# Attention on TensorE: which operand of the key-value products stands, and which moves

## The chip, the cores and the metric

The kernel runs on one core of a Trainium2 chip. The metric is the device time of one execution in microseconds (us). Before the change the median of three runs is 1320.67 us (1320.23 to 1321.27).

## The reference

Linear attention with exponential features, followed by two feed-forward mixtures that the change doesn't touch. Batch 4, 8 heads, 576 positions, head size 64, 128 features:

```python
def phi(x):
    proj = np.einsum('bhsd,df->bhsf', x, w_phi)
    proj = proj - np.max(np.abs(proj), axis=-1, keepdims=True)
    return np.concatenate([np.exp(proj), np.exp(-proj)], axis=-1)
q_p, k_p = (phi(q), phi(k))
kv = np.einsum('bhsf,bhsd->bhfd', k_p, v)
z = np.sum(k_p, axis=2)
num = np.einsum('bhsf,bhfd->bhsd', q_p, kv)
den = np.einsum('bhsf,bhf->bhs', q_p, z)[..., None] + 1e-06
return (num / den).astype(np.float32)
```

So each head needs a table kv (256 features by 64 values) and the sums z (256) of the key exponentials over all positions. All is f32.

## The kernel before, in words

The 32 heads are worked in 16 pairs. A pair's 576 positions are four blocks of 128 and a tail of 64; the tails of both heads share one tile. Per pair, TensorE projects keys and queries (`project`, L403, and `project_tails`, L410), VectorE finds the largest magnitude and subtracts it (`largest` L419, `less` L425), ScalarE takes both exponentials of the keys with positions on the partitions (`exp_keys` L430, `exp_tails` L435, tiles ke and ket). The queries are transposed on TensorE first (`turn_queries`, L500 and L503) and exponentiated with features on the partitions (`exp_queries`, L509 and L511, tile qe).

The key-value table comes in these steps:

- `key_values` (L447): 32 columns of v stand in one of four column strips of the array (two heads, two halves of the 64 values), the 256 exponentials of one block move. Values end on the partitions, features in the columns, in a PSUM tile kv of its own. It is issued in two parts (plan names KV-0 and KV-1).
- `sum_keys` (L470, L471; plan name Z): GpSimd or VectorE adds the four blocks of exponentials into zsum.
- `add_up` (L456; ZZ): ones stand and zsum and ket move, so the sums land beside the table.
- `save_kv` (L209 by the copy helper; CV): two copies of 256 columns out of PSUM into kvs.
- `turn_kv` (L484, L486; TV): four transposes on TensorE, since attention needs features on the partitions.
- `copy_kv` (L209; VH) and `add_halves` (L493; VZ): a copy of 384 columns to kvt, and an addition of two halves of the sums.

`attend` (L522; A) and `denominators` (L532; AD) take 32 columns of kvt as the standing operand and move qe. A chain on VectorE and ScalarE (D0 to X2) divides and writes Xh and Xl, the input of the first mixture. Blocks of that mixture (U and M, L292 and L313) are mixed into attention's order as soon as their input is there. The rest of the mixtures follows attention.

Instructions are issued by a planner (`Plan.run`). TensorE's order is the list ORDER, written out by hand; each entry is one step such as KV3-1. The other engines' orders come from the planner's booked costs, due times (RANK and SHIFT) and buffers; a step that two engines can do goes to the one that would end first by these costs. `SWITCH` holds the planner's booked costs for a change of array mode: row (two strips of 64 rows), quarter (four strips of 32 columns), full (f32 on the whole array) and rounded (fp32r on the whole array). Loads are issued from the DMA queue of SyncE in the planner's order (`load`, L390 to L394); v has one buffer of 128 x 512, vt two. PSUM has five shared banks (bank), one for kv and two for the mixture (mm).

Of the kernel before, what the change touches and what calls it, by code (L numbers as in the profile page):

```python
# [45 lines left out]
NZ = 0  # L46
# [10 lines left out]
    C=-146.759, CV0=109.999, CV1=-182.316, D0=-57.584, D1=-146.332, D2=39.304, D3=-224.318, E0=88.966,  # L57
    E1=41.132, E2=96.018, G0=208.743, G1=-173.239, G2=438.049, I=-129.377, N0=-51.099, N1=-127.846, Rk0=-43.022,
    Rk1=162.626, Rq0=-5.647, Rq1=132.286, Rt=-62.242, Sk0=-113.184, Sk1=7.061, Sq0=-463.551, Sq1=-197.328,
    St=-302.881, VH=16.756, VZ=-249.208, W=41.842, W3=73.288, W4=140.933, W5=-142.37, X0=255.513, X1=364.708,  # L60
    X2=383.376, Z0=266.794, Z1=165.123, ldk=-63.631, ldq=-41.539, ldv=10.731,
# [6 lines left out]
AD2 ZZ3 T3-1 TV3 Pk-4 A2-0 AD3 A2-1 PT4 Pq-4 Pk-5 A3-0 KV4-0 KV4-1 A3-1 Pq-5 ZZ4 T4-0 T4-1 TV4 KV5-0 T4-2
T5-0 T5-2 KV5-1 A4-0 A4-1 AD4 PT6 Pk-6 ZZ5 T5-1 U2-0 TV5 Pq-6 KV6-0 A5-0 KV6-1 AD5 A5-1 T6-0 T6-2 PT7 ZZ6
PT8 Pk-7 Pq-7 TV6 U0-0 T7-0 T6-1 U3-0 T7-1 T7-2 KV7-0 AD6 A6-0 KV7-1 PT9 ZZ7 Pk-8 Pq-8 TV7 U1-0 A6-1 A7-0  # L70
KV8-0 A7-1 KV8-1 AD7 ZZ8 Pk-9 Pq-9 T8-0 M0-1 T8-1 M0-3 TV8 T9-0 T8-2 T9-1 KV9-0 PT11 A8-0 AD8 KV9-1 PT10 ZZ9
T9-2 M0-2 M0-0 Pk-10 Pq-10 TV9 U2-1 U3-1 A8-1 AD9 KV10-0 A9-0 KV10-1 A9-1 ZZ10 Pk-11 Pq-11 T10-0 U0-1 TV10
T10-1 T11-0 U1-1 T11-2 T10-2 T11-1 KV11-0 PT13 KV11-1 AD10 ZZ11 Pq-12 Pk-12 TV11 M1-1 M1-3 M1-2 A10-0 PT12
KV12-0 A10-1 AD11 A11-0 KV12-1 A11-1 ZZ12 Pk-13 Pq-13 T12-0 M1-0 T12-1 T13-0 TV12 U3-2 T12-2 T13-1 T13-2
KV13-0 AD12 KV13-1 PT14 ZZ13 A12-0 Pq-14 Pk-14 TV13 U1-2 U0-2 U2-2 KV14-0 A12-1 KV14-1 PT15 ZZ14 AD13 Pk-15
Pq-15 T14-0 M2-3 M2-0 T14-2 T14-1 TV14 KV15-0 A13-0 KV15-1 A13-1 ZZ15 A14-0 TV15 T15-0 T15-1 T15-2 AD14
# [997 lines left out]
```

## Time and profile before

| | us |
|---|---|
| median of three runs | 1320.67 |
| the profiled execution, its own time | 1321.2 |
| its span, first to last instruction | 1319.1 |
| from the start to the end of attention's matmuls | 236.7 |

The profile is one execution. PE is TensorE's matmuls, PEld its weight loads, DVE VectorE, ACT ScalarE, POOL GpSimd, SP SyncE with the DMA queue. Matmuls overlap, so the busy time of PE is the time in which at least one is in flight, and the price of one is the distance from its start to that of the next. "128*32" is the part of the array an instruction uses (rows by columns), "128x256" the operand that moves, or, of a load, the operand that stands. An f32 matmul call is two loads and two matmul instructions.

### The profile page before, as it was taken

The numbers are of one execution on the slowest core, as the hardware profiler recorded it, in microseconds if no ns is written. First come the engines' busy times: TensorE is split into PE (matmuls) and PEld (weight loads), VectorE is DVE, ScalarE is ACT, GpSimd is POOL, SyncE is SP. The second block draws the span as 40 slices with busy tenths as digits, with TensorE's granted clock in tenths as the row PEclk, the third lists the DMA queues.
The fourth block names the chain that finished last, engine by engine and source line by source line (L and its number), as shares of the span: only waits on it lengthen the run. The fifth ranks groups of instructions, "written<-read, shape, count | busy, mean of one in ns | idle before, by whom it ended". The sixth has DMA issues, their size and how long they took to land.

```text
span 1319.1 us, 21240 instructions
## 1 busy us (share of the span) xinstructions
PE 1307.2 (99%) x8184; PEld 1118.5 (85%) x8184; DVE 758.1 (57%) x1283; ACT 454.6 (34%) x979; POOL 274.2 (21%) x292
## 2 busy tenths in 40 slices
PE   9999999999999999998999999999999999999998
PEld 5577776888888888897999998999999899999997
DVE  7996866999697456664455446433343453333433
ACT  6775655332131121253444433222222232222221
POOL 5562412120020130274566620000000000000000
PEclk9999999999999999999999999999999999999999
DMA  5431220322020030098677666666666565566641
GB/s 168 123 110 49 55 56 12 112 81 96 17 72 9 9 119 1 25 320 287 246 254 257 251 221 197 227 188 194 195 188 192 176 224 175 176 186 190 192 135 48
DMA packets 102469, 192.36 MB, mean 146 GB/s; under 512 B 13920, under 2 KB 14048, under 8 KB 102368
## 3 DMA queue, kind: packets, MB, share of 16 engines
q1 hardware_dynamic: 102368, 191.00, 44.5%
q8 instruction: 65, 1.06, 0.3%
q14 instruction: 36, 0.29, 0.1%
HBM read 140.10 MB, written 50.86 MB: 145 GB/s over the span
## 4 chain that ended last, share of the span: by engine, by line
PE 93%; DVE 3%; DMA 1%; ACT 1%; issue 1%; SPq 0%; POOL 0%; DVEq 0%; ACTq 0%; POOLq 0%
PE dn L981 29%; PE up L934 25%; PE up L292 12%; PE dn L313 12%; PE mm L313 3%; PE mm L292 2%; PE kv L447 2%; PE bank L522 2%; PE bank L403 2%; DVE m L419 1%; PE bank L532 1%; PE bank L503 1%; DMA w<-wdn 1%; PE kv L456 0%; DVE pmk L425 0%
## 5 line engine op out<-in xcount | busy, mean ns | idle before, releaser
L981 PE MATMUL dn<-whd,Xh 128*128 128x512 f32 x720 | 231.4, 390 | 0.0
L992 DVE SCALAR_TENSOR_TENSOR acc<-dn,pr,acc 128x512 f32<-128x512 f32 x126 | 88.7, 749 | 190.9 <-PE dn L981 190.9
L934 PE MATMUL up<-Xl,wlu 128*128 128x384 f32 x864 | 158.8, 335 | 2.7 <-DVE c L947 2.6
L981 PEld LDWEIGHTS dn<-whd,Xh 128*128 128x128 f32 x720 | 135.1, 188 | 27.1
L934 PEld LDWEIGHTS up<-Xl,wlu 128*128 128x128 f32 x864 | 150.2, 188 | 4.3 <-DVE c L947 3.8
L947 DVE TENSOR_TENSOR c<-up,p 128x384 f32<-128x384 f32 x96 | 53.5, 557 | 174.1 <-PE up L934 171.5
L981 PE MATMUL dn<-Xh 128*128 128x512 f32 x648 | 151.8, 389 | 0.0
L981 PEld LDWEIGHTS dn<-Xh 128*128 128x128 f32 x648 | 121.6, 188 | 25.5
L981 PE MATMUL dn<-wld,Xh 128*128 128x512 f32 x360 | 140.8, 391 | 0.0
L952 ACT COPY p<-up 128x384 f32<-128x384 f32 x48 | 23.1, 481 | 325.7 <-PE up L934 325.6
L934 PE MATMUL up<-Xl,whu 128*128 128x384 f32 x576 | 111.7, 334 | 1.1 <-ACT p L952 1.1
L941 ACT ACTIVATE Xh<-c 128x384 fp32r<-128x384 f32 x144 | 75.6, 526 | 80.0 <-DVE c L947 80.0
L934 PEld LDWEIGHTS up<-Xl,whu 128*128 128x128 f32 x576 | 101.2, 188 | 1.4 <-ACT p L952 1.4
L292 PE MATMUL up<-Xl,whu 128*128 128x512 f32 (+1 forms) x272 | 99.1, 364 | 0.0
L292 PE MATMUL up<-Xh,whu 128*128 128x512 f32 (+1 forms) x272 | 99.1, 364 | 0.0
L313 PE MATMUL dn<-gh,wld 128*128 128x512 f32 (+1 forms) x272 | 99.1, 364 | 0.0
L313 PE MATMUL dn<-gh,whd 128*128 128x512 f32 (+1 forms) x272 | 99.1, 364 | 0.0
L313 PE MATMUL dn<-gl,whd 128*128 128x512 f32 (+1 forms) x272 | 99.0, 364 | 0.0
L292 PE MATMUL up<-Xh,wlu 128*128 128x512 f32 (+1 forms) x272 | 99.0, 364 | 0.0
L942 DVE SCALAR_TENSOR_TENSOR Xh<-c,Xh 128x384 fp32r<-128x384 f32 x144 | 86.0, 599 | 5.4
L237 ACT CAST gh<-t 128x512 fp32r<-128x512 f32 (+1 forms) x68 | 38.6, 569 | 145.1 <-DVE t L304 143.0
L981 PEld LDWEIGHTS dn<-wld,Xh 128*128 128x128 f32 x360 | 67.5, 188 | 13.0
(171 smaller groups left out, 2222.4 us busy)
## 6 DMA issues: line engine op xcount, KB each, us to landing
whu<-wsu SPq DMA_DIRECT2D x96, 256.0 KB, 3.4
wlu<-wsu SPq DMA_DIRECT2D x96, 256.0 KB, 3.1
st<-w SPq DMA_DIRECT2D x24, 512.0 KB, 3.2
wsu<-whu SPq DMA_DIRECT2D x48, 256.0 KB, 3.1
wsu<-wlu SPq DMA_DIRECT2D x48, 256.0 KB, 2.3
Xh<-wsd SPq DMA_DIRECT2D x48, 256.0 KB, 3.8
wld<-wsd SPq DMA_DIRECT2D x40, 256.0 KB, 3.0
whd<-wsd SPq DMA_DIRECT2D x40, 256.0 KB, 3.3
```

The source lines that it names most:

```text
L237: nc.scalar.copy(hi, src)
L292: nc.tensor.matmul(ps[:, :bn], a[:, cs], x[:, cc, t0:t0 + bn], start=n == 0, stop=n == 3 * CC - 1)
L313: nc.tensor.matmul(ps, w[:, sl], g, start=start and k == 0, stop=stop and k == 2)
L403: nc.tensor.matmul(ps[h][:, i], x[r, i * P:(i + 1) * P], w0[r, h], start=True, stop=True, tile_position=(h * D, 0), skip_group_check=True)
L447: nc.tensor.matmul(kv[h * D + o:h * D + o + 32, 0], a[:, o:o + 32], e, start=i == 0, stop=i == NM, tile_position=(0, h * D + o), skip_grou ...
L522: nc.tensor.matmul(nd[o:o + 32, :HS], tl["kvt", p][:, a:a + 32], tl["qe", p][:, h, s, c * HS:(c + 1) * HS], start=s == 0, stop=s == 1, til ...
L934: nc.tensor.matmul(ps[name], w[k][:, r, kt * P:(kt + 1) * P], slots[k][:, x + kt], start=start and n == 0, stop=stop and n == 5, skip_grou ...
L941: nc.scalar.activation(gh, src, AF.Relu)
L942: nc.vector.scalar_tensor_tensor(gl, src, 0.0, f32(gh), ALU.max, ALU.subtract)
L947: nc.vector.tensor_tensor(o, ps[name], x, ALU.add)
L981: nc.tensor.matmul(ps[m], x[:, sl], w, start=c == chunks[0] and k == 0, stop=c == chunks[-1] and k == 2)
L992: nc.vector.scalar_tensor_tensor(av, ps[m], pe, av, ALU.mult, ALU.add)
```

## The change

The operands change places. The 128 features of one sign of one block (from ke or ket) stand in the full array, and the 64 values and 32 columns of ones move, 96 columns (DZ). So the table and the sums come out with features on the partitions at once, in a shared bank laid out as sign, head, 96 columns. The steps KV-0 and KV-1 are now one head each, with eight products (four blocks, two signs), and KV-2 is both tails with four. `sum_keys`, `add_up`, `save_kv`, `turn_kv` and `add_halves` go, and with them kvs, zsum, ones and the kv bank; `copy_kv` is one copy of 4 x 96 columns to kvt. The ones are written once, behind the values in two fixed buffers for v and two for vt; v now lands in runs of 64 values. Shared banks go from five to six. The planner books 896, 896 and 448 ns for the three KV steps. SHIFT has new numbers throughout, and ORDER is a new list of 216 steps in place of 232, whose first and last lines stand below; by it the array changes mode 73 times in place of 100, and the tail projections of pair 1 (PT1) come third, before the queries of pair 0 (Pq-0).

```diff
--- before.py
+++ after.py
@@ -34,6 +34,7 @@
 NM = S // P
 TL = S - NM * P
 HS = S // 2
+DZ = D + 32
 
 BLK2 = 384
@@ -43,7 +44,6 @@
 EP = NF2 // 2
 SEQ = (1, 5, 6, 2, 7, 3, 4)
 NA = 3
-NZ = 0
 AHEAD = 2
 
@@ -54,27 +54,26 @@
 WSTEP = 0.46
 
 SHIFT = dict(
...
 )
 
 ORDER = """
-Pk-0 Pq-0 PT0 Pk-1 KV0-0 T0-0 KV0-1 PT1 Pq-1 ZZ0 T0-1 T0-2 PT2 KV1-0 TV0 T1-0 T1-1 AD0 Pk-2 KV1-1 A0-0 ZZ1
...
-A14-1 A15-0 AD15 A15-1 M2-1 M2-2
+Pk-0 PT0 PT1 Pk-1 Pq-0 KV0-0 KV0-1 Pq-1 KV0-2 T0-0 KV1-0 T0-2 T0-1 KV1-2 KV1-1 T1-0 AD0 Pk-2 A0-0 A0-1 T1-1
...
+KV14-2 T15-0 T15-2 KV15-0 T15-1 KV15-1 KV15-2 M2-1 A14-0 A15-0 AD15 A14-1 AD14 A15-1 M2-0 M2-2
 """.split()
 
 BIAS = dict(v=1560, a=447, p=940)
@@ -345,20 +344,20 @@
             plan.bufs[name] = bufs
 
         for args in (
-            ("kr", 2, F32, P, S), ("qr", 2, F32, P, S), ("v", 1, F32, P, NM, 2, D),
+            ("kr", 2, F32, P, S), ("qr", 2, F32, P, S),
             ("m", 13, F32, P, 4), ("pmk", 2, F32, P, NM, F), ("pmq", 2, F32, P, NM, F), ("pmt", 2, F32, P, 2, F),
             ("ke", 3, F32, P, NM, 2, F), ("ket", 2, F32, P, 2, F),
-            ("kvs", 1, F32, P, 4, F), ("qe", 2, F32, P, 2, 2, S), ("kvt", 2, F32, P, 3 * P),
+            ("qe", 2, F32, P, 2, 2, S), ("kvt", 2, F32, P, 2, 2, DZ),
             ("dt", 1, F32, P, HS), ("di", 2, F32, P, HS // 32, 1), ("dj", 2, F32, P, S // 32, 1),
             ("rb", 1, F32, P, S), ("num", 2, F32, P, S),
-            ("zsum", 2, F32, P, 2, 2 * F), ("gh", 4, F32R, P, BLK), ("gl", 4, F32R, P, BLK), ("t", 2, F32, P, BLK),
+            ("gh", 4, F32R, P, BLK), ("gl", 4, F32R, P, BLK), ("t", 2, F32, P, BLK),
         ):
             ring(*args)
-        ring("bank", 5, F32, P, 512, space=PSUM)
-        ring("kv", 1, F32, P, 2, 2 * F, space=PSUM)
+        ring("bank", 6, F32, P, 512, space=PSUM)
         ring("mm", 2, F32, P, BLK, space=PSUM)
-        ones = pool("ones", 1, st1).tile([P, 3, 32], F32, name="ones")
-        vts = [pool(f"vt{i}", 1, st1).tile([P, 2, D], F32, name=f"vt{i}") for i in range(2)]
+        vs = [pool(f"v{i}", 1, st1).tile([P, NM, 2, DZ], F32, name=f"v{i}") for i in range(2)]
+        vts = [pool(f"vt{i}", 1, st1).tile([P, 2, DZ], F32, name=f"vt{i}") for i in range(2)]
+        plan.bufs["v"] = 2
         plan.bufs["vt"] = 2
         one = const.tile([P, 1], F32, name="one")
         eps = const.tile([P, 1], F32, name="eps")
@@ -387,9 +386,9 @@
         def load(p, n):
             b, j = pairs[p]
             if n == "v":
-                nc.sync.dma_start(new("v", p), v_main[b, j])
+                nc.sync.dma_start(vs[p % 2][:, :, :, :D], v_main[b, j])
                 for h in range(2):
-                    nc.sync.dma_start(vts[p % 2][h * TL:(h + 1) * TL, h], v_tail[b, j, h])
+                    nc.sync.dma_start(vts[p % 2][h * TL:(h + 1) * TL, h, :D], v_tail[b, j, h])
             else:
                 nc.sync.dma_start(new(n + "r", p), (qT if n == "q" else kT)[b, j])
 
@@ -437,60 +436,17 @@
         flat = lambda x: x.rearrange("p i s f -> p i (s f)")
         tail = lambda x: x.rearrange("p s f -> p (s f)")
 
-        def key_values(p, part):
-
-            kv = new("kv", p) if part == 0 else tl["kv", p]
-            for i in ((0, 1), (2, 3, 4))[part]:
-                for h in range(2):
-                    a, e = (tl["v", p][:, i, h], flat(tl["ke", (p, h)])[:, i]) if i < NM else (vts[p % 2][:, h], tail(tl["ket", p]))
-                    for o in range(0, D, 32):
-                        nc.tensor.matmul(kv[h * D + o:h * D + o + 32, 0], a[:, o:o + 32], e, start=i == 0, stop=i == NM,
-                                         tile_position=(0, h * D + o), skip_group_check=True)
-
-        def add_up(p):
-
-            kv = tl["kv", p]
-
-            def product(par, h, a, e, stop):
-                r = 32 * (2 * par + h)
-                nc.tensor.matmul(kv[r:r + 32, 1], a, e, start=False, stop=stop, tile_position=(0, r), skip_group_check=True)
-
-            for h in range(2):
-                if p >= NZ:
-                    product(0, h, ones[:, 0], tl["zsum", (p, h)][:, 0], True)
-                    continue
-                for i in range(NM):
-                    product(i % 2, h, ones[:, 0], flat(tl["ke", (p, h)])[:, i], i == 2)
-            for h in range(2):
-                product(1, h, ones[:, 1 + h], tail(tl["ket", p]), True)
-
-        def sum_keys(p, h, e):
-            ke = flat(tl["ke", (p, h)])
-            z = new("zsum", (p, h))
-            engines[e].tensor_tensor(z, ke[:, :2], ke[:, 2:], ALU.add)
-            engines[e].tensor_tensor(z[:, 0], z[:, 0], z[:, 1], ALU.add)
-
-        def save_kv(p, k, e):
-            kvs = (new if k == 0 else lambda *x: tl[x])("kvs", p).rearrange("p (k s) f -> p k (s f)", k=2)
-            cp(engines[e], kvs[:, k], tl["kv", p][:, k])
-
-        def turn_kv(p):
-
-            kvs = tl["kvs", p].rearrange("p (k s) f -> p k s f", k=2)
-            b = new("bank", ("kv", p))
-            new("kvt", p)
-            z = b[:, 2 * P:].rearrange("p (a s c) -> p a s c", a=2, s=2)
-            for s in range(2):
-                nc.tensor.transpose(b[:, s * P:(s + 1) * P], kvs[:, 0, s], ident)
-            for s in range(2):
-                nc.tensor.transpose(z[:, :, s], kvs[:, 1, s], ident)
+        def key_values(p, n):
+
+            kv = (new if n == 0 else lambda *x: tl[x])("bank", ("kv", p))[:, :4 * DZ].rearrange("p (s h d) -> p s h d", s=2, h=2)
+            for h in range(2) if n == 2 else (n,):
+                for i in range(NM) if n < 2 else (NM,):
+                    for s in range(2):
+                        a, e = (vs[p % 2][:, i, h], tl["ke", (p, h)][:, i, s]) if n < 2 else (vts[p % 2][:, h], tl["ket", p][:, s])
+                        nc.tensor.matmul(kv[:, s, h], e, a, start=(h, i, s) == (0, 0, 0), stop=i == NM, skip_group_check=True)
 
         def copy_kv(p, e):
-            cp(engines[e], tl["kvt", p], tl["bank", ("kv", p)][:, :3 * P])
-
-        def add_halves(p):
-            o = tl["kvt", p][:, 2 * P:]
-            nc.vector.tensor_tensor(o, tl["bank", ("kv", p)][:, 3 * P:], o, ALU.add)
+            cp(engines[e], new("kvt", p), tl["bank", ("kv", p)][:, :4 * DZ].rearrange("p (s h d) -> p s h d", s=2, h=2))
 
         def turn_queries(p, h):
             ps = new("bank", ("qt", p, h))
@@ -518,8 +474,7 @@
             for s in range(2):
                 for o in range(0, P, 32):
                     to, h = divmod(o // 32, 2)
-                    a = s * P + h * D + to * 32
-                    nc.tensor.matmul(nd[o:o + 32, :HS], tl["kvt", p][:, a:a + 32],
+                    nc.tensor.matmul(nd[o:o + 32, :HS], tl["kvt", p][:, s, h, to * 32:to * 32 + 32],
                                      tl["qe", p][:, h, s, c * HS:(c + 1) * HS], start=s == 0, stop=s == 1,
                                      tile_position=(0, o), skip_group_check=True)
 
@@ -529,7 +484,7 @@
                 for h in range(2):
                     for c in range(2):
                         r = 32 * (2 * c + h)
-                        nc.tensor.matmul(nd[r:r + 32, :HS], tl["kvt", p][:, 2 * P + s * D + h * 32:2 * P + s * D + (h + 1) * 32],
+                        nc.tensor.matmul(nd[r:r + 32, :HS], tl["kvt", p][:, s, h, D:],
                                          tl["qe", p][:, h, s, c * HS:(c + 1) * HS], start=s == 0, stop=s == 1,
                                          tile_position=(0, r), skip_group_check=True)
 
@@ -589,30 +544,12 @@
                    reads=[("pmk", (p, h))], emit=lambda e, a=(p, h): exp_keys(*a))
             op(("E", p, 2), {"a": 2 * act(F)}, [("S", "t", p)], RANK["E"] + p + 0.2, alloc=[("ket", p)],
                reads=[("pmt", (p,))], emit=lambda e, p=p: exp_tails(p))
-            es = [("E", p, h) for h in range(2)]
-            kes = [("ke", (p, h)) for h in range(2)]
-            op(("KV", p, 0), {"t": pe32(2 * F, 2)}, [*es, ("ld", "v", p)], RANK["KV"] + p, alloc=[("kv", p)], mode="quarter",
-               emit=lambda e, p=p: key_values(p, 0))
-            op(("KV", p, 1), {"t": pe32(2 * F, 3)}, [("KV", p, 0), ("E", p, 2)], RANK["KV"] + p + 0.1, reads=[*kes, ("ket", p), ("v", p), ("vt", p)],
-               mode="quarter", emit=lambda e, p=p: key_values(p, 1))
-            zs = []
-            if p >= NZ:
-                zs = [("Z", p, h) for h in range(2)]
-                for h in range(2):
-                    op(("Z", p, h), {"v": dve(512) + dve(256), "p": gps(512) + gps(256)}, [("E", p, h)], RANK["Z"] + p, port=True, alloc=[("zsum", (p, h))],
-                       reads=[("ke", (p, h))], emit=lambda e, a=(p, h): sum_keys(*a, e))
-            op(("ZZ", p), {"t": pe32(2 * F, 1 if p >= NZ else 3)}, [("KV", p, 1), *zs], RANK["TV"] + p,
-               reads=[("zsum", (p, h)) for h in range(2)] + [("ket", p)] if zs else [*kes, ("ket", p)], mode="quarter",
-               emit=lambda e, p=p: add_up(p))
-            for k in range(2):
-                op(("CV", p, k), copy_cost(256), [("ZZ", p) if k else ("KV", p, 1)], RANK["TV"] + p, alloc=[("kvs", p)] if k == 0 else [],
-                   behind=[("CV", p, 0)] * k, reads=[("kv", p)], emit=lambda e, a=(p, k): save_kv(*a, e))
-            op(("TV", p), {"t": 436}, [("CV", p, 0), ("CV", p, 1)], RANK["TV"] + p, alloc=[("bank", ("kv", p))],
-               reads=[("kvs", p)], mode="full", emit=lambda e, p=p: turn_kv(p))
-            op(("VH", p), copy_cost(3 * P), [("TV", p)], RANK["TV"] + p, alloc=[("kvt", p)],
+            for n in range(3):
+                op(("KV", p, n), {"t": (896, 896, 448)[n]}, [("E", p, n), ("ld", "v", p)], RANK["KV"] + p + 0.1 * n, alloc=[("bank", ("kv", p))] * (n == 0),
+                   behind=[("KV", p, 0)] * (n > 0), reads=[("v", p), ("vt", p), ("ket", p)] if n == 2 else [("ke", (p, n)), ("v", p)], mode="full",
+                   emit=lambda e, a=(p, n): key_values(*a))
+            op(("VH", p), copy_cost(4 * DZ), [("KV", p, n) for n in range(3)], RANK["TV"] + p, alloc=[("kvt", p)],
                reads=[("bank", ("kv", p))], emit=lambda e, p=p: copy_kv(p, e))
-            op(("VZ", p), {"v": dve(P)}, [("VH", p)], RANK["TV"] + p,
-               reads=[("bank", ("kv", p))], emit=lambda e, p=p: add_halves(p))
             for h in range(3):
                 pr_ = RANK["Q"] + p + 0.1 * h
                 pm, n = (("pmt", (p,)), 1) if h == 2 else (("pmq", (p, h)), NM)
@@ -629,7 +566,7 @@
                    emit=lambda e, a=(p, c): attend(*a))
                 op(("N", p, c), copy_cost(HS), [("A", p, c)], pr_,
                    reads=[("bank", ("n", p, c))], emit=lambda e, a=(p, c): take(*a, e))
-            op(("AD", p), {"t": pe32(HS, 2)}, [*xs, ("VH", p), ("VZ", p)], RANK["A"] + p + 0.2, reads=[("qe", p), ("kvt", p)],
+            op(("AD", p), {"t": pe32(HS, 2)}, [*xs, ("VH", p)], RANK["A"] + p + 0.2, reads=[("qe", p), ("kvt", p)],
                alloc=[("bank", ("d", p))], mode="quarter", emit=lambda e, p=p: denominators(p))
             pr_ = RANK["F"] + p
             op(("D0", p), {"v": 370}, [("AD", p)], pr_, alloc=[("dt", p)],
@@ -736,14 +673,16 @@
             for _ in range(4):
                 nc.tensor.matmul(o[:32, :2 * F], busy[:, :32], busy, start=True, stop=True)
             nc.gpsimd.memset(w0, 0.0)
-            nc.gpsimd.memset(ones, 1.0)
             nc.gpsimd.memset(eps, 1e-6)
             for h in range(2):
                 nc.sync.dma_start(w0[h * D:(h + 1) * D, h], w_phi)
-                nc.gpsimd.memset(ones[h * D:(h + 1) * D, 2 - h], 0.0)
             for x in vts:
                 nc.gpsimd.memset(x, 0.0)
-            nc.scalar.copy(one, ones[:, 0, :1])
+                for h in range(2):
+                    nc.gpsimd.memset(x[h * TL:(h + 1) * TL, h, D:], 1.0)
+            for x in vs:
+                nc.gpsimd.memset(x[:, :, :, D:], 1.0)
+            nc.scalar.copy(one, eps)
             make_identity(nc, ident)
             nc.sync.dma_start(alpha_sb, alpha)
             plan.run()
```

## Rows read from the trace of the kernel before

**Rows 1.** The page's chain that ended last, shares of the span by engine.

```profile
PE 93%; DVE 3%; DMA 1%; ACT 1%; issue 1%; SPq 0%; POOL 0%; DVEq 0%; ACTq 0%; POOLq 0%
```

**Rows 2.** Busy time by stretch: length, PE, PEld, DVE, ACT, POOL, clock, DMA, GB/s.

```profile
236.70:1319.10 1082.40, 1074.78 (x5377) 954.57 (x5375) 573.62 (x938) 302.51 (x616) 178.85 (x200) 1.00 0.48 159
...
0.00:20.00 20.00, 17.60 (x209) 11.39 (x213) 13.61 (x27) 11.75 (x28) 9.43 (x21) 1.00 0.65 204
20.00:80.00 60.00, 58.91 (x858) 38.46 (x857) 57.79 (x114) 46.26 (x115) 33.64 (x28) 1.00 0.42 125
80.00:236.70 156.70, 155.89 (x1754) 114.10 (x1747) 113.06 (x207) 94.04 (x223) 52.25 (x45) 1.00 0.19 53
```

**Rows 3.** Timeline of PE within 100 to 125 us: start, length, instruction, count.

```profile
104.91 1.05 PE L447 MATMUL kv<-ke,v 128*32 128x256 f32 x16
...
106.20 1.15 PE L532 MATMUL bank<-qe,kvt 128*32 128x288 f32 x16
107.17 0.39 PE L456 MATMUL kv<-zsum,ones 128*32 128x256 f32 x2
...
107.72 1.16 PE L403 MATMUL bank<-w,kr 64*128 64x128 f32 x16
108.71 1.06 PE L403 MATMUL bank<-w,qr 64*128 64x128 f32 x16
...
116.24 0.38 PE L484 MATMUL bank<-ident,kvs 128*128 128x128 f32 x2
116.46 0.38 PE L486 MATMUL bank<-ident,kvs 128*128 128x128 f32 x2
```

**Rows 4.** Groups by line, 0 to 300 us: weight loads; busy us, mean ns.

```profile
L447 PEld LDWEIGHTS kv<-ke,v 128*32 128x32 f32 x512 | 15.8, 109 | 11.2 <-issue 2.0 <-ACT ke L430 0.6
L403 PEld LDWEIGHTS bank<-w,qr 64*128 64x128 f32 x256 | 15.6, 188 | 3.5 <-issue 2.0 <-DMA qr<-qT 0.7 <-DVE pmk L425 0.4
L503 PEld LDWEIGHTS bank<-ident,pmq 128*128 128x128 f32 x128 | 14.3, 140 | 4.8 <-issue 1.7 <-ACT num L209 0.4 <-DVE pmt L425 0.4
```

**Rows 5.** Timeline of PE behind attention: full-array fp32r steps, 256 and 512 columns.

```profile
247.46 0.28 PE L292 MATMUL up<-Xh,whu 128*128 128x256 f32 x1
...
248.77 0.28 PE L292 MATMUL up<-Xh,wlu 128*128 128x256 f32 x1
...
298.02 0.39 PE L292 MATMUL up<-Xl,whu 128*128 128x512 f32 x1
...
299.84 0.39 PE L292 MATMUL up<-Xh,whu 128*128 128x512 f32 x1
```

**Rows 6.** Timeline of the start, several engines; SPq is the DMA queue's issue.

```profile
1.19 3.62 PE L737 MATMUL mm<-acc_a 128*32 128x256 f32 x8 [1.19 <-DVE acc_a L734]
...
1.57 0.36 POOL L745 MEMSET vt<- 128x128 f32 x2
...
3.51 0.91 SPq L394 DMA_DIRECT2D qr<-qT  x2
...
7.02 1.16 PE L403 MATMUL bank<-w,qr 64*128 64x128 f32 x16 [0.54 <-DMA qr<-qT]
```

**Rows 7.** Groups by line, 0 to 300 us: work on the other engines that goes.

```profile
L470 POOL TENSOR_TENSOR zsum<-ke 128x512 f32<-128x512 f32 x23 | 30.8, 1338 | 65.5 <-ACT ke L430 63.3 <-PE kv L456 2.3
...
L209 ACT COPY kvs<-kv 128x256 f32<-128x256 f32 x32 | 11.9, 374 | 10.1 <-PE kv L447 5.9 <-PE kv L456 3.8
...
L470 DVE TENSOR_TENSOR zsum<-ke 128x512 f32<-128x512 f32 x9 | 6.5, 727 | 3.1 <-ACT ke L430 3.1
...
L493 DVE TENSOR_TENSOR kvt<-bank,kvt 128x128 f32<-128x128 f32 x16 | 4.5, 280 | 1.5 <-ACT kvt L209 1.3
```

**Rows 8.** DMA issues (KB each, median us to landing) and the DMA queue's waits.

```profile
qr<-qT SPq DMA_DIRECT2D x16, 288.0 KB, 3.2
...
v<-v_main SPq DMA_DIRECT2D x16, 256.0 KB, 2.7
...
SPq L390 <- PE kv L447: 104.2, 15, 13.6
```

More of the change, by code (lines that the diff above doesn't have):

```diff
@@ L56 @@
 SHIFT = dict(
[L57 to L61, printed above, removed]
+    C=-203.07, D0=-32.72, D1=-162.037, D2=21.023, D3=-291.685, E0=77.613, E1=31.226, E2=91.483, G0=323.541,
@@ L62 @@
+    G1=-124.017, G2=477.635, I=-245.344, N0=-108.818, N1=-146.593, Rk0=-84.994, Rk1=136.313, Rq0=-73.583,
+    Rq1=166.762, Rt=31.722, Sk0=-157.622, Sk1=-35.864, Sq0=-465.758, Sq1=-146.946, St=-238.309, VH=13.387,
+    W=40.006, W3=18.728, W4=190.598, W5=-111.057, X0=175.517, X1=385.981, X2=399.657, ldk=-20.944, ldq=-11.731,
+    ldv=-3.372,
 )
 ORDER = """
-Pk-0 Pq-0 PT0 Pk-1 KV0-0 T0-0 KV0-1 PT1 Pq-1 ZZ0 T0-1 T0-2 PT2 KV1-0 TV0 T1-0 T1-1 AD0 Pk-2 KV1-1 A0-0 ZZ1
-Pq-2 A0-1 PT3 TV1 T2-0 T1-2 KV2-0 A1-0 AD1 KV2-1 Pk-3 ZZ2 A1-1 Pq-3 TV2 T2-1 T2-2 KV3-0 T3-0 PT5 T3-2 KV3-1
@@ L68 @@
[L68 to L76, printed above, removed]
-A14-1 A15-0 AD15 A15-1 M2-1 M2-2
+Pk-0 PT0 PT1 Pk-1 Pq-0 KV0-0 KV0-1 Pq-1 KV0-2 T0-0 KV1-0 T0-2 T0-1 KV1-2 KV1-1 T1-0 AD0 Pk-2 A0-0 A0-1 T1-1
@@ new lines @@
+Pq-2 T1-2 PT3 A1-0 PT2 AD1 T2-0 T2-1 KV2-0 KV2-2 T2-2 Pk-3 KV2-1 A1-1 Pq-3 AD2 A2-0 PT4 T3-0 KV3-0 T3-2 T3-1
+KV3-2 KV3-1 PT5 Pk-4 A3-0 AD3 A3-1 Pk-5 A2-1 KV4-0 KV4-1 Pq-5 Pq-4 KV4-2 KV5-0 KV5-2 T5-0 T5-1 KV5-1 T4-0
+T4-2 T4-1 T5-2 U0-0 AD4 A5-0 A4-0 A5-1 PT7 PT6 Pk-6 A4-1 AD5 Pq-6 Pk-7 U1-0 T6-0 U2-0 Pq-7 T6-1 KV7-0 KV6-0
+KV7-2 KV6-1 KV6-2 T6-2 T7-0 T7-2 T7-1 KV7-1 U3-0 PT9 PT8 A7-0 A7-1 A6-0 AD7 A6-1 AD6 Pk-8 Pq-8 Pk-9 M0-3
+M0-1 M0-0 M0-2 Pq-9 T8-0 T8-1 KV8-0 KV8-1 T9-0 T9-2 T8-2 KV9-0 KV8-2 KV9-1 KV9-2 PT10 A8-0 AD8 A8-1 Pq-10
@@ new lines @@
+Pk-10 T9-1 U0-1 U3-1 U1-1 A9-0 PT11 AD9 A9-1 Pk-11 Pq-11 T10-0 T10-1 U2-1 KV11-0 T10-2 KV10-0 KV10-1 KV11-2
+T11-0 T11-2 KV10-2 KV11-1 T11-1 M1-1 PT13 A11-0 A11-1 AD10 PT12 A10-0 A10-1 AD11 Pq-12 Pk-13 Pk-12 M1-0 M1-3
+M1-2 KV13-0 Pq-13 KV13-2 T12-0 KV13-1 KV12-0 KV12-2 T12-1 KV12-1 T13-0 T12-2 T13-2 U1-2 U2-2 A12-0 AD12 PT14
+A12-1 Pq-14 Pk-14 T13-1 U0-2 U3-2 T14-0 AD13 PT15 A13-0 A13-1 Pk-15 Pq-15 KV14-0 T14-1 KV14-1 T14-2 M2-3
+KV14-2 T15-0 T15-2 KV15-0 T15-1 KV15-1 KV15-2 M2-1 A14-0 A15-0 AD15 A14-1 AD14 A15-1 M2-0 M2-2
```

## The prediction

> **What bounds the kernel now.** I read the chain that ended last first: it lies on TensorE for 93% of the span [rows 1]. Then the stretches: attention ends at about 236.7 us, the two mixtures behind it take the other 1082.4 us, and the diff touches nothing there [rows 2]. Inside attention TensorE is busy 17.60 of the first 20 us, 58.91 of the next 60 and 155.89 of the last 156.7, at a granted clock of 1.00. VectorE is nearly as full only from 20 to 80 us (57.79 of 60) and falls to 113 of 156.7 afterwards [rows 2]. So a microsecond more or less of TensorE work per pair is a microsecond per pair in the end, except for the little idle time there is. A matmul's own duration is no price, since matmuls overlap; prices are distances between starts in the timeline.
>
> **What is removed on TensorE.** Per pair of heads: the second half of key_values, 24 instructions from 104.91 to 106.20, 1.29 us; the first half has 16 of the same, 0.86 us; add_up has eight, 0.43 us; turn_kv has four transposes, of which the first two take from 116.24 to 116.46, so 0.44 us in all [rows 3]. That is 3.02 us, over 16 pairs 48.3 us.
>
> **What is added on TensorE.** key_values now makes 20 products per pair (four blocks and a tail, two heads, two signs), each with 128 x 128 exponentials standing and 96 columns moving. One f32 product is two loads and two matmuls: the old loop makes 16 calls per pair on ke, 256 in all, and 512 loads are listed [rows 4]. So there are 40 load and matmul steps per pair, 640 in all. No row shows a full-array f32 step that is not a transpose, so its price is bounded.
> From below by the stream of columns: 24 instructions of 256 columns, four side by side, took 1.29 us [rows 3], which is 0.84 ns per column; 96 columns take 0.081 us.
> By the load: an f32 load of 32 columns takes 109 ns, one of 128 columns (the projections') 188 ns, so each column costs (188 - 109) / 96 = 0.82 ns and 128 columns occupy the load path for 0.105 us [rows 4].
> From above: full-array fp32r steps of 256 columns, each with a load of 128 columns, follow each other at (248.77 - 247.46) / 11 = 0.119 us, and 512 columns at (299.84 - 298.02) / 8 = 0.2275 us [rows 5]; the difference gives 0.108 us for 256 columns, so about 0.011 us of each step is a handoff. The projections, 16 instructions from 107.72 to 108.71, two side by side, need 0.124 us per two [rows 3]; that is my upper bound.
> I take 0.112 us, halfway between the bare load (0.105) and the nearest row (0.119). 640 x 0.112 = 71.7 us, 23.4 us more than the 48.3 removed. Streaming 96 instead of 256 columns doesn't help, since loading 128 columns is then the longer half, and the old form loads 32.
>
> **Fewer changes of array mode.** By the two written orders, the old one passes 100 times from one mode to another (quarter, row, full, rounded) and the new one 73 times. From quarter to row costs 0.12 us (add_up starts at 107.17, has 0.43 us of work, and the next begins at 107.72) [rows 3]; other changes may cost less, down to nothing. 27 at 0.07 us, a little over half: 1.9 us saved, ends 0 and 3.2.
>
> **Idle time that added work can fill, and relief elsewhere.** TensorE idles 2.4 us in the first 20 us, of which 1.19 lie before its first instruction [rows 6], 1.1 us in the next 60 and 0.8 us in the rest [rows 2]: 3.1 us at most. ScalarE loses 32 copies of 374 ns (12 us). GpSimd loses the sums of keys, 23 first steps of 1338 ns (30.8 us) and as many second ones; VectorE loses nine of the same, 6.5 us by the first step alone, and 16 additions of 280 ns, 4.5 us [rows 7]. None of this is on the path where TensorE is full; from 20 to 80 us it lets VectorE feed TensorE sooner. I take 2 us saved, ends 0 and 3.1.
>
> **Start.** The new order puts the tails of pair 1 in third place, before the queries of pair 0. They need both loads of pair 1. The two q loads are issued from 3.51 to 4.42 us and take 3.2 us, so they land at about 7.6, where TensorE went on at 7.02 [rows 6, 8]: 0.6 us added, ends 0 and 1.
>
> **Costed at nothing.** The copy of kvt still moves 384 columns on ScalarE. The extra fills on GpSimd (vt's two took 0.36 us, from 1.57; there are now four small ones more and two of twice the size, less three, so about 1 us) lie beside TensorE's opening matmuls, which end at 4.81 [rows 6]; without that cover they would cost that 1 us. The v load now writes runs of 256 bytes instead of 2 KB per partition; that costs between nothing and a second landing of 2.7 us [rows 8]. It also gets a second buffer: the DMA queue stood 104.2 us on the single one, behind the key matmuls, with the k, q and weight loads queued behind it [rows 8]. That hides the longer landing for all pairs but the first; if the cover went, each pair could pay up to 2.7 us. Earlier loads can save waits like the 0.54 us at 7.02 [rows 6], for which I book nothing. The new chain (products, one copy, attend) is shorter than the old one (products, two copies, transposes, copy, addition); the key products now hold a shared bank until the copy, one of six instead of one of five plus their own, which I count as even.
>
> **Sum.** 23.4 - 1.9 - 2.0 + 0.6 = 20.1 us more; the last three together take off 3.3. The profiled execution took 1321.2 us (its span 1319.1 and 2.1 around it), 0.5 above the median of 1320.67; so 1341.3 against it and, taken from the median, 1340.8, which I round to 1341.
>
> **The rivals.** (a) Load-paced, the forecast: 1341, chance 0.68; with 0.105 to 0.124 us and the ends of the small terms, 1333 to 1353.
> (b) The loads run as fast as those of the f32 transposes (140 ns where the others take 188 [rows 4]), and the stream with its handoff, 0.081 + 0.011, sets the pace: 0.092 x 640 = 58.9, 10.6 - 3.3 = 7.3 more, 1328. For it: the same full-array shape and type. Against it: f32 projections, which are no transposes, load in 188. Chance 0.13.
> (c) The stream alone, 0.081: 51.8, 3.5 - 3.3 = 0.2 more, 1321; with the best of every small term (6.3 in all) 1318. No row with a load of 128 columns shows so small a handoff. Chance 0.07.
> (d) Faster: the steps cost what the changed plan books, 896 ns for eight products, 0.056 us each. 35.8 us, so 12.5 + 3.3 = 15.8 us are saved, 1305. It needs a stream at the 0.42 ns per column of the fp32r rows [rows 5], 0.040 us, and a load half as long as the durations say, both in key_values. The f32 rows speak against the stream. It decides from (48.3 + 3.3 - 2.6) / 640 = 0.077 us per step downwards. Chance 0.10.
> (e) Loads that cannot run beside a matmul of the same rows: 0.105 + 0.081 = 0.186 us per step, 119.0 us, 70.7 - 3.3 = 67.4 more, 1388. The rows at 0.119 us, with a load of 0.105 and a stream of 0.108 in each, show both side by side in the full array; it would have to be peculiar to f32 in two halves. Chance 0.02.
> The Trainium skill, "TensorE: Matmul & The Clock Gate", Part 3 (what overlaps and what doesn't), says that a weight load overlaps matmuls in flight only where it goes to other row groups, which speaks against this change and is (e); by it the time would be 1388, by the rows 1341. The rows of 256 columns contradict it for the full array, as far as fp32r goes.
> VectorE as the pace of the first 80 us would hide the added 1.46 us of some five pairs there, 7 us, and give 1334; TensorE's 58.91 of 60 us speaks against it, and it lies inside the range.
>
> **Range and chances.** The range holds (a), (b) and (c), from 1318 (stream alone and every small gain) to 1350 (every step at 0.119 and no gain: 27.9 + 0.6 more, 1349). About 0.2% or 2.6 us is what a measurement of this kernel can tell from no change. Slower: 0.68 + 0.11 of (b) + 0.02 = 0.81; same: 0.02 of (b) and 0.04 of (c), 0.06; faster: 0.10 and 0.03 of (c), 0.13.
>
> **What the changed profile would show.** Right: the key products' starts are 0.105 to 0.119 us apart in the timeline, 4.2 to 4.8 us per pair; attention ends 17 to 25 us later; TensorE stays at 98% there; the sums of keys, kvs and add_halves are gone and GpSimd's share falls. Wrong, if the starts are under 0.09 us apart (loads no bound), if TensorE shows new idle time beside key products or their copy (a bank or the copy is late), or if the time after attention changes.

## The result: about 1% slower, by less than the forecast

The changed kernel takes 1333.89 us (median of four runs, 1333.54 to 1334.08), 1.0096 times the kernel before (1320.97 us over four runs), interval 1.0079 to 1.0114. Its profiled execution took 1334.07 us with a span of 1332.3, 13.2 us more than the span before.

The chain that ended last, from the page of the changed kernel, which answers to [rows 1]:

```profile
PE 97%; DMA 1%; SPq 0%; POOL 0%; issue 0%; DVE 0%; ACT 0%; POOLq 0%; DVEq 0%; ACTq 0%
PE dn L920 29%; PE up L873 25%; PE up L291 12%; PE dn L312 12%; PE bank L446 5%; PE mm L312 3%; PE mm L291 2%; PE bank L477 2%; PE bank L402 2%; PE bank L487 1%; PE bank L459 1%; DMA w<-wdn 1%; PE bank L409 1%; DMA wsu<-whu 0%; DMA qr<-qT 0%
```

Busy time by stretch of the changed kernel (length, PE, PEld, DVE, ACT, POOL, clock, DMA, GB/s; compare [rows 2]). The first product of the next mixture starts at 251.75 us, where it started at 236.54:

```profile
0.00:20.00 20.00, 17.53 (x178) 14.03 (x179) 12.59 (x24) 10.01 (x22) 2.49 (x16) 1.00 0.74 219
20.00:80.00 60.00, 60.00 (x772) 46.99 (x773) 47.36 (x95) 42.54 (x104) 26.68 (x20) 1.00 0.42 117
80.00:251.70 171.70, 171.70 (x1674) 140.92 (x1671) 98.59 (x182) 89.03 (x205) 34.94 (x26) 1.00 0.17 44
251.70:1332.30 1080.60, 1075.02 (x5377) 954.75 (x5376) 574.52 (x939) 304.09 (x618) 180.00 (x200) 1.00 0.49 160
```

VectorE fell from 57.79 to 47.36 of the 60 us between 20 and 80, GpSimd from 33.64 to 26.68, and TensorE is busy in all 60. The stretch behind attention is 2 us shorter. The new products in the timeline of the changed kernel (start, length, instruction, count), then their loads in the groups by line:

```profile
89.14 3.71 PE L446 MATMUL bank<-v,ke 128*128 128x96 f32 x32
92.69 1.06 PE L446 MATMUL bank<-vt,ket 128*128 128x96 f32 x8
93.58 1.95 PE L446 MATMUL bank<-v,ke 128*128 128x96 f32 x16
```

```profile
L446 PEld LDWEIGHTS bank<-v,ke 128*128 128x128 f32 x512 | 59.4, 192 | 1.0 <-ACT dj L508 0.5
```

32 steps from 89.14 to 92.69 are 0.111 us each; a load lasts 192 ns. 640 steps take 71.0 us, against about 48.4 for the instructions that went.

**Where 13.2 us come from.** I priced every instruction of attention by the distance between starts in an undisturbed stretch of its kind, and took what is left between starts as changes of array mode and waits. The counts of changes stand in brackets; full f32 and fp32r are one mode here, so there are 75 and 58 in place of the 100 and 73 of the written orders.

| TensorE until attention ends, us | before | after |
|---|---|---|
| instructions at their price | 218.3 | 242.2 |
| at changes of mode | 9.4 (75) | 5.2 (58) |
| within a mode | 4.0 | -0.4 |
| before the first projection | 4.7 | 4.7 |

So instructions cost 24 us more (22.6 of it the exchange itself, the rest the coarseness of the prices), 8.6 us of changes and waits went, attention ends 15.2 us later, and 2 us come back behind it. How much is called a wait hangs on the prices: with the median distance between starts of equal instructions as the price throughout, 18.8 us are left before and 10.8 after. What went, 8.0 us, is nearly the same.

### The profile page after: what moved, and what is told of

Same layout as the page of the kernel before. It is cut to its first block, busy times and chain, and to the rows that moved or that the text cites. A ratio compares the mean times of both kernels' runs of the same rounds, so it can differ in the third digit from the quotient of the medians.

```text
span 1332.3 us, 20734 instructions
## 1 busy us (share of the span) xinstructions
PE 1324.3 (99%) x7992; PEld 1156.7 (87%) x7992; DVE 733.1 (55%) x1237; ACT 445.7 (33%) x947; POOL 244.1 (18%) x261
## 4 chain that ended last, share of the span: by engine, by line
PE 97%; DMA 1%; SPq 0%; POOL 0%; issue 0%; DVE 0%; ACT 0%; POOLq 0%; DVEq 0%; ACTq 0%
PE dn L920 29%; PE up L873 25%; PE up L291 12%; PE dn L312 12%; PE bank L446 5%; PE mm L312 3%; PE mm L291 2%; PE bank L477 2%; PE bank L402 2%; PE bank L487 1%; PE bank L459 1%; DMA w<-wdn 1%; PE bank L409 1%; DMA wsu<-whu 0%; DMA qr<-qT 0%
```

## The experiments

e1, e2, e3, e5, e6, e10 and e11 are one run each; the others have four or more. On the chips used, the medians of the kernel before were 1320.6 to 1321.8 us, and its runs lay up to 2.8 us from them, so a difference of 1 or 2 us between single runs says little. In the diffs, `...` marks lines left out.

### What paces a key product

Three edits of the one call: fewer moving columns, more of them, fewer standing ones.

```diff
+w = DZ if i == 0 else D
-nc.tensor.matmul(kv[:, s, h], e, a, start=(h, i, s) == (0, 0, 0), stop=i == NM, skip_group_check=True)
+nc.tensor.matmul(kv[:, s, h, :w], e, a[:, :w], start=(h, i, s) == (0, 0, 0), stop=i == NM, skip_group_check=True)
```

> Changed kernel, but only the first block of each head moves the 32 columns of ones; 512 of the 640 key-product steps move 64 columns in place of 96 (the sums of the other blocks and of the tails are left out). Theory, the steps wait for the load of 128 standing columns: starts stay 0.111 us apart, time 1333 to 1335. Rival, the moving columns set the pace: 512 x 32 x 0.84 ns = 13.8 us less, about 1320.

```diff
+w = P if n < 2 and (i, h) != (3, 1) else DZ
+if w == P:
+    k = (2 * i + h) * DZ
+    a = vs[p % 2].rearrange("p i h d -> p (i h d)")[:, k:k + P]
-nc.tensor.matmul(kv[:, s, h], e, a, start=(h, i, s) == (0, 0, 0), stop=i == NM, skip_group_check=True)
+nc.tensor.matmul(kv[:, s, h, :w], e, a, start=(h, i, s) == (0, 0, 0), stop=i == NM, skip_group_check=True)
...
```

> Changed kernel, with 128 columns moving (32 of them of no use and never read) in 14 of the 20 products of a pair, 448 steps of 640. Theory, load-paced at 96: the stream now takes 0.108 us, and with a handoff of 0.011 the starts go from 0.111 to 0.119 us, 448 x 0.008 = 3.6 us more, about 1337.5. Rival, paced by the stream with a large fixed handoff (0.081 + 0.030): 0.138 us, 12 us more, about 1346.

```diff
+m = P if i == 0 else P // 2
-nc.tensor.matmul(kv[:, s, h], e, a, start=(h, i, s) == (0, 0, 0), stop=i == NM, skip_group_check=True)
+nc.tensor.matmul(kv[:m, s, h], e[:, :m], a, start=(h, i, s) == (0, 0, 0), stop=i == NM, skip_group_check=True)
```

> Changed kernel, but beyond the first block only 64 of the 128 features stand (the other half of the table is left out there), 512 of 640 steps. Theory, load-paced: a load of 64 columns needs about 0.052 us, the stream of 96 becomes the longer, starts about 0.092 us apart, 512 x 0.019 = 9.7 us less, about 1324, plus up to 3 for array changes. Rival, paced by the stream with a large handoff: starts stay at 0.111, 1334.

Timeline of e1 (tails and three blocks in four move 64 columns):

```profile
88.75 3.68 PE L447 MATMUL bank<-v,ke 128*128 128x96 f32 x32
92.27 1.06 PE L447 MATMUL bank<-vt,ket 128*128 128x64 f32 x8
```

Timeline of e2 (blocks move 128 columns):

```profile
89.06 3.74 PE L450 MATMUL bank<-v,ke 128*128 128x128 f32 x32
92.63 1.03 PE L450 MATMUL bank<-vt,ket 128*128 128x96 f32 x8
```

Timeline of e3 (a group holds four full steps and twelve with 64 standing columns, a tail eight of these):

```profile
126.83 1.72 PE L447 MATMUL bank<-v,ke 128*128 128x96 f32 x16
128.38 0.82 PE L447 MATMUL bank<-vt,ket 128*64 128x96 f32 x8
129.13 1.82 PE L447 MATMUL bank<-v,ke 128*128 128x96 f32 x16
```

Moving 64 columns (in three of four steps) gives (92.27 - 88.75) / 32 = 0.110 us a step, 96 gave 0.111, 128 gives 0.1116; inside the groups the starts are 0.112 us apart in all three traces. The times are 1332.69 and 1334.17. So up to 128 moving columns cost nothing beside the load of 128 standing ones. The handoff that I expected to come on top in e2 doesn't: 0.1116, not 0.119.

Half the standing columns give 0.75 / 8 = 0.094 us with a change of mode in it (128.38 to 129.13). Between the changes the starts in this trace are 0.0825 us apart, which is the stream alone, 0.86 ns for each of 96 columns. The time is 1329.54, only 4.4 us less, since e3 now changes mode inside each group: from full steps to half ones 0.205 us pass in place of 0.112, back 0.176 in place of 0.083.

So with 128 columns standing, something other than the stream sets the pace, and with 64 it no longer does. The load is the reading that fits, by size too (0.105 us estimated). One rival stays: e3 changes the array mode together with the standing columns, so a fixed floor of 0.11 us for f32 steps in the full array is not excluded. No run had, say, 96 columns standing in the full mode.

### Narrower strips, and fewer moving columns

```diff
-nc.tensor.matmul(kv[:, s, h], e, a, start=(h, i, s) == (0, 0, 0), stop=i == NM, skip_group_check=True)
+for o in range(0, P, 32):
+    nc.tensor.matmul(kv[o:o + 32, s, h], e[:, o:o + 32], a, start=(h, i, s) == (0, 0, 0), stop=i == NM,
+                     tile_position=(0, o), skip_group_check=True)
```

> Changed kernel, whole computation, but the 128 features stand as four strips of 32 columns, each its own call (four times the calls). It passes between array modes 105 times in place of 73, some 3 us. Theory A, the loads of the four strips pass one after the other: four take 0.105 us as before, time 1333 to 1338. Theory B, the strips load side by side and the stream sets the pace at about 0.081 to 0.085 us per four: 640 x 0.028 = 18 us less and 3 more, about 1319, below both kernels.

e7 has the same with strips of 64:

```diff
-for o in range(0, P, 32):
-    nc.tensor.matmul(kv[o:o + 32, s, h], e[:, o:o + 32], a, start=(h, i, s) == (0, 0, 0), stop=i == NM,
+for o in range(0, P, 64):
+    nc.tensor.matmul(kv[o:o + 64, s, h], e[:, o:o + 64], a, start=(h, i, s) == (0, 0, 0), stop=i == NM,
                      tile_position=(0, o), skip_group_check=True)
```

> Changed kernel, whole computation, but the 128 features stand as two strips of 64 columns (twice the calls, half those of the four strips). Theory, two strips stream side by side and load side by side, so the 96 moving columns set the pace at 0.082 us per two: 640 x 0.029 = 18 us less, 3 more for array modes, and no wait for instructions as with four strips: about 1319, at or below the kernel before. Rival, strips of 64 don't overlap: 0.082 us each, 34 us more, about 1368.

and e8 adds to e7:

```diff
-DZ = D + 32
+DZ = D + 4
...
-cp(engines[e], new("kvt", p), tl["bank", ("kv", p)][:, :4 * DZ].rearrange("p (s h d) -> p s h d", s=2, h=2))
+t = new("kvt", p)
+kv = tl["bank", ("kv", p)][:, :4 * DZ].rearrange("p (s h d) -> p s h d", s=2, h=2)
+cp(engines[e], t[:, :, :, :D], kv[:, :, :, :D])
+cp(engines[e], t[:, :, :, D:], kv[:, :, :, D:D + 1].to_broadcast([P, 2, 2, 32]))
...
```

> As e7, but only four columns of ones move (68 columns in all) and the copy spreads the sum over 32 columns, as a second copy on ScalarE. Theory, the stream sets the pace: 68 x 0.84 = 0.057 us per two, 640 x 0.054 = 34 us less than the changed kernel, 3 more for array modes: about 1303. Rival, the loads of 64 columns (0.052 us) with a handoff, or the issue of instructions, stop it at 0.07 to 0.08: 1311 to 1318.

| | step of 128 features, us | time, us | ratio to before, interval |
|---|---|---|---|
| changed kernel | 0.111 | 1333.89 | 1.0096, 1.0079 to 1.0114 |
| e4, four strips | 0.0825 | 1327.05 (1325.55 to 1330.26) | 1.0043, 1.0026 to 1.0060 |
| e7, two strips | 0.0825 | 1321.62 | 1.0002, 0.9993 to 1.0011 |
| e8, two strips, 68 columns | 0.0594 | 1307.68 | 0.9900, 0.9879 to 0.9921 |

Timelines of e7 and, below, of e8 (each step is now two instructions):

```profile
87.49 1.49 PE L447 MATMUL bank<-v,ke 128*64 128x96 f32 x32
88.81 0.83 PE L447 MATMUL bank<-vt,ket 128*64 128x96 f32 x16
```

```profile
81.59 1.12 PE L447 MATMUL bank<-v,ke 128*64 128x68 f32 x32
82.54 0.64 PE L447 MATMUL bank<-vt,ket 128*64 128x68 f32 x16
```

In strips the loads no longer set the pace, and the stream does: 1.32 us for 16 steps of 96 columns is 0.86 ns per column, 0.95 us for 16 steps of 68 is 0.87. In e8 the loads of 128 columns, as two strips, pass in 0.0594 us where the full array takes 0.111. I read this as loads side by side; that each strip loads faster by itself would look the same here. So columns of ones that cost nothing in the full array cost 0.023 us a step in strips, and dropping 28 of them is worth 14 us. e8 is 1% faster than the kernel before.

e7 stands nearly 3 us above its forecast: attention ends 12 us earlier than in the changed kernel for 18 us less of steps, because it changes mode 99 times in place of 58, for 11.2 us in place of 5.2. e8 stands 5 us above its forecast; it has the same 99 changes (11.8 us) and steps of 0.0594 in place of 0.057 us.

e4 has the same steps as e7. Its profile is of the slowest of its four runs, 1330.26 us, 8 us above the profile of e7. TensorE's waits in it for instructions are 5.1 us (engine, line, what ended it, us in total, times, longest):

```profile
PE bank L402 <- issue: 3.5, 1, 3.5
PE bank L447 <- issue: 1.6, 2, 0.9
```

In the longest of these waits the granted clock fell from 1.00 to 0.50, the lower level (1.2 GHz). Steps of four strips then started 0.160 us apart in place of 0.083, and by such prices the slow stretch cost another 3.4 us. How much of both the other three runs have, 1325.55 to 1328.53, is not shown.

### Where the 8.6 us of waits and mode changes went

Two theories: the new order of TensorE, or the work taken from VectorE and GpSimd. Up to 1.0 us may belong to neither: so long add_up, a step that is gone, waited in the kernel before for the copies out of the kv bank (`PE kv L456 <- ACT kvs L209: 1.0, 4, 0.4` among PE's waits). e5 puts the old order back. The steps of every pair are rewritten as here those of pair 1; this is the rule, and the steps between them in the list are left out:

```diff
-KV1-0 ZZ1 TV1
-KV1-1
+KV1-0 KV1-1
+KV1-2
```

> Changed kernel with TensorE's order of before: each old KV-0 becomes the new KV-0 and KV-1, each old KV-1 the new KV-2, ZZ and TV fall out. It changes array mode 118 times in place of 73. Theory, the 8.6 us of idle time and mode changes that went in attention went by the new order: 45 changes at 0.08 us give 3.6 us back and waits beside them 1 to 5, 1338 to 1343. Rival, they went because the other engines were relieved: the order gives only part of the mode changes back, 1334 to 1337.

e6 puts unread sums back, behind the exponentials, into one buffer (zsum had two before); e10 and e11 do so on one engine alone, 24 on GpSimd or 8 on VectorE:

```diff
...
-("gh", 4, F32R, P, BLK), ("gl", 4, F32R, P, BLK), ("t", 2, F32, P, BLK),
+("zsum", 1, F32, P, 2, 2 * F), ("gh", 4, F32R, P, BLK), ("gl", 4, F32R, P, BLK), ("t", 2, F32, P, BLK),
...
+g = nc.vector if (2 * p + h) % 4 == 3 else nc.gpsimd
+z = new("zsum", (p, h))
+x = e.rearrange("p i s f -> p i (s f)")
+g.tensor_tensor(z, x[:, :2], x[:, 2:], ALU.add)
+g.tensor_tensor(z[:, 0], z[:, 0], z[:, 1], ALU.add)
```

> Changed kernel, with the sums of keys put back as work of which nothing is read: 24 on GpSimd and 8 on VectorE, behind the exponentials. Theory, order made the difference: within 1.5 us of 1333.9. Rival, the relief of GpSimd and VectorE made it: 3 to 6 us more, 1337 to 1340.

> As e6, but only the 24 unread sums on GpSimd come back. Theory, VectorE's own time from 20 to 80 us is what feeds TensorE: less than half of the 11 us of e6, 1335 to 1339. Rival, work behind the sums in GpSimd's queue is what TensorE waits for: 1341 to 1345.

> As e6, but only the eight unread sums on VectorE come back (8 x 1.29 us, half of them before 80 us). Theory, VectorE's own time counts: 3 to 6 us more than the changed kernel, 1337 to 1340. Rival: under 1.5 us more.

And e9 takes the sums out of the kernel before:

```diff
-product(0, h, ones[:, 0], tl["zsum", (p, h)][:, 0], True)
+product(0, h, ones[:, 0], flat(tl["ke", (p, h)])[:, 0], True)
...
 def sum_keys(p, h, e):
-    ke = flat(tl["ke", (p, h)])
-    z = new("zsum", (p, h))
-    engines[e].tensor_tensor(z, ke[:, :2], ke[:, 2:], ALU.add)
-    engines[e].tensor_tensor(z[:, 0], z[:, 0], z[:, 1], ALU.add)
+    pass
...
-reads=[("zsum", (p, h)) for h in range(2)] + [("ket", p)] if zs else [*kes, ("ket", p)], mode="quarter",
+reads=[("zsum", (p, h)) for h in range(2)] + [*kes, ("ket", p)], mode="quarter",
```

> Kernel before, with the sums of keys on GpSimd and VectorE left out (the plan and its orders unchanged; the ones multiply the first block alone, so the sums of three blocks are missing). TensorE's instructions are the same. Theory, relief of VectorE and GpSimd lets TensorE wait less: of some 6 us of waits that are not mode changes 2 to 5 go, 1316 to 1319. Rival, relief alone gives nothing, the order has to be written for it: 1320 to 1322.

The last column is the time from the first projection (at 4.7 us; 4.35 in e6, 4.49 in e11) to the end of attention, less the price of the instructions from the table above, which is the same for all runs of one kernel. Time at a lower clock is in it too.

| | time, us | attention ends at, us | mode changes and waits in attention, us |
|---|---|---|---|
| changed kernel | 1333.89 | 251.75 | 4.8 |
| e5, old order | 1348.20 | 266.69 | 19.7 |
| e6, all sums back | 1345.07 | 263.14 | 16.6 |
| e10, on GpSimd alone | 1335.09 | 252.62 | 5.7 |
| e11, on VectorE alone | 1337.03 | 255.58 | 8.9 |
| kernel before | 1320.97 | 236.54 | 13.5 |
| e9, before without sums | 1324.11 (1.0017, 1.0007 to 1.0027) | 238.20 | 15.2 |

Waits of PE, longest of e6 and of e11:

```profile
PE bank L464 <- DVE pmq L424: 6.1, 2, 3.8
```

```profile
PE bank L466 <- DVE pmq L424: 2.6, 1, 2.6
```

TensorE waits in both to transpose queries from which VectorE has not yet subtracted the maxima. Eight sums on VectorE cost the changed kernel 3.1 us, 24 on GpSimd 1.2, both together 11.2, above both forecasts of e6.

**Why e6 is no sum of e10 and e11.** First, in e6 VectorE's sums wait for GpSimd's sums to leave the single buffer, which neither the kernel before nor e10 or e11 has. The queries' maxima stand behind them in VectorE's queue:

```profile
DVE zsum L433 <- POOL zsum L434: 11.3, 4, 5.1
```

Second, the granted clock falls in or right behind TensorE's two long waits; its mean from 20 to 80 us is 0.91. Key products at 1.00 and at 0.50, 16 steps each, and below them the stretch from 73 to 78 us:

```profile
67.69 1.95 PE L451 MATMUL bank<-v,ke 128*128 128x96 f32 x16
74.53 3.57 PE L451 MATMUL bank<-v,ke 128*128 128x96 f32 x16
```

```profile
73.00:78.00 5.00, 5.00 (x25) 5.00 (x25) 4.08 (x8) 2.12 (x5) 2.09 (x2) 0.50 0.00 0
```

The next steps start at 69.48 and 77.89, so the 16 took 1.79 us at the full clock and 3.36 at half of it. By the starts inside the slow stretches, 0.213 us a step in place of 0.112, the lower clock cost e6 about 4.5 us, and e5, e11 and e12 about 1.6 us each, behind waits of 2.1 to 3.8 us. In the changed kernel and the kernel before the clock stays at 1.00 through attention.

So e6 says little of the relief. e11 shows that VectorE's time matters in the new order, but 3.1 us is more than the price of the work: part is the clock, and its sums stand in VectorE's queue waiting for exponentials, 11.7 us in all where those of the kernel before waited 3.1 [rows 7]. e10's 1.2 us lies within the spread of single runs.

In the old order relief gained nothing in e9: the kernel before without its sums is slightly slower, though VectorE is busy 53.81 us from 20 to 80 in place of 57.79:

```profile
20.00:80.00 60.00, 59.09 (x870) 37.38 (x868) 53.81 (x103) 46.39 (x115) 25.56 (x19) 1.00 0.42 127
```

But this is no clean test either. add_up now reads the key exponentials, the planner holds them until then, and in the trace ScalarE, VectorE and GpSimd run their steps in another order than in the kernel before, against what I had expected.

e5 lost 14 us, above both of its forecasts. About 5 us are waits for VectorE and ScalarE, 1.6 the clock, and the rest lies mainly at changes of mode. That is no clean price of the order, since the due times of the other engines (SHIFT) are those of the new one and the planner gave them other orders.

What the runs support: of the 8.6 us about 4 are changes of mode that went (9.4 to 5.2), up to 1.0 were add_up's waits, and e11 makes it likely that some of the rest hangs on VectorE's relief. How the rest is shared between order, relief, the second buffer of v and the sixth bank stays open. That each list of TensorE's steps holds for the other engines' work that it was written beside fits e5 and e12, but is not shown by itself.

e12 asked the same of e8: wherever transposes and key products stand next to each other, all of one kind first, as in this stretch of the order.

```diff
-KV0-2 T0-0 KV1-0 T0-2 T0-1 KV1-2 KV1-1 T1-0
+KV0-2 KV1-0 KV1-2 KV1-1 T0-0 T0-2 T0-1 T1-0
```

> As e8, but where transposes of queries and key products stand next to each other in TensorE's order, all of one kind come first, then all of the other: 72 changes of array mode in place of 99, the same work. Theory, a change between these two modes costs 0.12 to 0.16 us: 3.2 to 4.3 us less, about 1304. Rival, the grouping makes products or transposes wait for exponentials or banks as the old order did in e5, and the gain is gone: 1307 to 1312.

1315.56 us, 0.9959 of before (0.9945 to 0.9973), so 8 us worse than e8 and above both forecasts. The changes of mode fell from 11.8 to 7.2 us as expected, but the rest rose from 1.3 to 12.2. Of that 1.6 us is the lower clock behind the longest wait (0.82 from 84 to 88 us, 0.76 from 88 to 92). This wait is in the timeline of e12:

```profile
85.14 0.63 PE L463 MATMUL bank<-ident,pmq 128*128 128x128 f32 x4 [3.66 <-DVE pmq L423]
```

## Why the prediction was right, point by point

**Direction and mechanism held.** "TensorE work per pair is a microsecond per pair in the end": attention ends 15.2 us later, with TensorE full. The signs held in part: the starts are 0.111 us apart, and no wait shows beside key products or their copy, but 15.2 us lies below the 17 to 25 given, and the time after attention changed.

**The price of a step held.** 0.112 us booked, 0.111 measured, 23.4 us booked and 22.6 found. That the stream is not the pace was argued then and is shown by e1 and e2; that the load is fits e3 and its size. The term of 0.011 us for a handoff, half of which was in the 0.112, was a chance hit: f32 steps show 0.110 to 0.112 at 64, 96 and 128 columns, so what stands above the estimated 0.105 is no addition to the stream. The trace of before held a nearer price: its full-array f32 transposes of 128 columns follow each other at 0.22 / 2 = 0.11 us [rows 3]. The 0.124 of the projections, the upper bound, has a change of mode in it; inside that group pairs start 0.112 us apart.

**The small terms were sized wrong**, and make nearly all of the miss of 7 us. "TensorE idles ... 3.1 us at most" failed: it took idle time from the busy share, which counts each matmul's whole flight and so covers short waits. Between starts there were 13.5 us of waits and mode changes (18.8 by the other pricing), and 8.6 of them went (8.0), where 1.9 and 2.0 were booked: changes gave 4.2, above the end of 3.2, waits 4.4, above the end of 3.1. The start, booked at 0.6 us more, cost nothing net: the same reckoning gives 4.0 us in the first 20 us before and 2.0 after, though PE does wait there for q as I said:

```profile
PE bank L409 <- DMA qr<-qT: 1.3, 2, 1.1
```

**"The time after attention changes" came true**, a sign of being wrong by the prediction's own words. It is 2 us shorter, where nothing was booked. PE's waits in the second mixture fell; before and, below, after:

```profile
PE up L934 <- DVE c L947: 2.6, 1, 2.6
PE up L934 <- ACT p L952: 1.1, 1, 1.1
```

```profile
PE up L873 <- DVE c L886: 1.2, 1, 1.2
PE up L873 <- ACT p L891: 0.4, 1, 0.4
PE up L873 <- ACT u L897: 0.2, 1, 0.2
```

e9, with the old layout, shows 3.5 us of these waits; e6, with the new one, 1.2. What moves them was not tried and stays open.

**The rivals.** (d) fell with the step at 0.111: eight products take 16 x 0.111 = 1.78 us where the plan books 0.896. (e) fell too, 0.111 against 0.186: a load and the matmul before it overlap on the same rows. The Trainium skill, "TensorE: Matmul & The Clock Gate", Part 3, in its list of what overlaps, would have loads wait there unless they go to other row groups; for full-array f32 this case measures otherwise. (b) and (c), the stream as the pace, are true only in strips (e7, e8); in the full array the loads take 192 ns, not the 140 that (b) needed.

The rival of VectorE as the pace of the first 80 us gave 1334, the measured time. That is a chance hit in the main: TensorE is busy in all of the 60 us behind the first 20, VectorE in 47.36. Something of it is true, since waits before did hide added work there: by the median pricing 8.0 us from 20 to 80 us before and 4.0 after, so 4 of the 8 us that went, where the rival hid 7 (the two stretches hold nearly the same steps, not quite). And (a)'s own upper end, 1353, lies outside the range of 1350, which didn't matter.

**Costed at nothing.** The first projection starts 4.7 us in as before, so the extra fills did cost nothing. The v load lands in 3.3 us in place of 2.7, and no wait of TensorE for v shows.

## What to carry to other kernels

As far as this kernel shows, price an f32 matmul on the full array by the longer of two: its standing columns at about 0.82 to 0.87 ns each, its moving columns at 0.84 to 0.87. Before exchanging operands, ask which of the two is then the longer; when it is the load, cut the standing side into strips, whose loads passed in about half the time here (e8), and then trim the moving side, which only now counts. The Trainium skill, "TensorEngine Tiling (Array Packing)", Performance Considerations, advises for a moving side of at most 64 columns to swap the operands and tile columns, as the old kernel did with its 64 values; here the exchange without strips lost to that by 1%, and with two strips and 68 columns beat it by 1%.

Idle time of an engine that is nearly full is read from start to start, not from its busy share.

Before the time of a run that puts work back is read as the price of that work, look at what its new instructions wait for and at the granted clock. In e6 a shared buffer and the lower clock were in it.
